# Prelu for the weights' words, v by pairs, zero products on the tensor engine and the softmax's factor on GpSimd

## The chip, the cores and the metric

One core of one Trainium2 chip runs the whole program. The metric is device time in microseconds of one execution, the median over the runs.

## The reference, cut to what matters

An attention layer whose heads are mixed before and after the softmax, followed by two dense pairs of layers. Sizes: 2 batches, 12 heads, 448 positions, head width 64; then 896 rows of 768, inner width 2048.

```python
scores = scale * np.matmul(q, k.transpose(0, 1, 3, 2))
scores = np.einsum('bhij,hg->bgij', scores, w_pre)
scores = scores - np.max(scores, axis=-1, keepdims=True)
attn = np.exp(scores)
attn = attn / (np.sum(attn, axis=-1, keepdims=True) + 1e-09)
attn = np.einsum('bhij,hg->bgij', attn, w_post)
return np.matmul(attn, v)
...
h = x @ w_in                              # first pair
g = np.where(h > 0.0, h, alpha * (np.exp(np.minimum(h, 0.0)) - 1.0))
y = g @ w_out
h = y @ w2_in                             # second pair
g = h * (1.0 / (1.0 + np.exp(-h)))
return g @ w2_out
```

The dense layers' weights arrive as float64: each is two 32-bit words, and the chip has to make a float32 of them before it can multiply.

## The kernel before, in words

The program has two stages, written out by hand in the order in which each engine is to run it.

**Attention.** The 896 rows of queries are cut into 8 tiles T (four per batch, of up to 120 rows), each tile into blocks of 10 rows; there are 90 blocks. Scores of a tile are made per pair of heads (`qk_pair`, tile `pq`), moved to SBUF (`qk_evac`, `s`) and from there laid out anew by a DMA per block (`relayout`, `blk`), so that 10 rows of 12 heads stand on 120 partitions. A block then goes through: `premix` on TensorE (mix with w_pre, tile `pre`), `rmax` on VectorE (`nmx`), `exps` on ScalarE (`pe`, with the row sums `sum`), `recip` on VectorE (add 1e-9, reciprocal, and `kr`, which is the post-mix matrix times the reciprocal: the softmax's factor), `postmix` on TensorE with `kr` (tile `post`), `post_hi` on ScalarE and `post_lo` on VectorE (two float16 parts, tile `a`). After a tile, `av_head` multiplies with v. v is also held in two float16 parts, which need a common scale: `v_max` takes a maximum per pair of heads, `v_scale` makes the scale of them in three steps (with two small matmuls, `vpa` and `vpb`), `prep_v` makes the parts: the high on ScalarE, the low either on VectorE (`v_lo`) or, in two operations, on GpSimd. `av_swap` sends half of a result to the other partitions by DMA and `av_sum` adds it, on GpSimd.

A loop over steps s records, in each step, `premix` of block s, `recip` of s-1, `postmix` of s-2 and `post_hi`, `post_lo` of s-3. Every engine works off its own list in order, so an instruction that waits holds all behind it on its engine. What else goes into a step stands in tables of steps: V_AT for v's work, P_AT for the two small matmuls, D_AT for DMAs (all issued by SP, also in order). Step 0 begins when the first tile's scores are made. Buffers: three PSUM banks for `pre`, two for `post`, one pair of banks for `pq`; five `blk`; two `s`.

**Dense layers.** From the last tile on, weights come in chunks: `load_w`, `scale_w` (ScalarE scales the high word), `bits_w` (VectorE joins the words by shifts and masks), `split_hi` on ScalarE and `split_lo` make two parts of 768 columns. The first three chunks (`n < NE`) are converted during the attention's last tile, with the tile `early` as their buffer, and their `split_lo` runs on GpSimd; all others on VectorE. Each product takes three matmuls (hi·hi, hi·lo, lo·hi).

The names in the rows: `vraw` and `vr` are raw v, `vmx` its maxima, `wr` and `wc` weights before and after the joining, `we` their parts, `ph`, `po`, `py` the products of the dense layers, `ptq` and `ptk` transposes of q and k, `xs`, `xt`, `xr` the attention's result.

## Time and profile before

| | |
|---|---|
| median of 3 runs | 743.95 us (743.8 to 744.45) |
| the profiled execution | 746.99 us, of which the span is 745.2 us |
| TensorE matmul | 722.4 us busy, 97% |
| TensorE weight load | 616.4 us, 83% |
| VectorE | 516.2 us, 69% |
| ScalarE | 398.1 us, 53% |
| GpSimd | 74.7 us, 10% |

The page divides the span into 40 slices of 18.6 us; digits are tenths. Matmuls overlap, so that the row of TensorE is at 9 even where single matmuls wait a little. Attention takes about the first 272 us; the last tile's result and the first dense products meet at about 270 to 282 us; from there to the end the dense layers run.

### The profile page before, as it was taken

How to read it: one execution, taken by the hardware profiler on the slowest of the kernel's cores; microseconds unless marked ns; L12 is line 12 of the kernel's file. 1: busy time of each engine (PE TensorE's matmuls, PEld its weight loads, DVE VectorE, ACT ScalarE, POOL GpSimd, SP SyncE). 2: the span in 40 equal slices, each digit the busy share in tenths (PEclk: the TensorE clock that was granted, in tenths of full speed). 3: DMA queues.
4: the chain of work that ended last, by engine and by line, in shares of the span. 5: the costliest groups of instructions: out<-in, count | busy, mean ns of one | idle time of the engine just before them, and what ended most of it. 6: DMA issues, size and time to landing. Idle time of an engine off the chain costs nothing.

```text
span 745.2 us, 12122 instructions
## 1 busy us (share of the span) xinstructions
PE 722.4 (97%) x4472; PEld 616.4 (83%) x4472; DVE 516.2 (69%) x1147; ACT 398.1 (53%) x789; POOL 74.7 (10%) x99
## 2 busy tenths in 40 slices
PE   7889999999998899999999999999999999999998
PEld 4456766776775688999999999999999999999997
DVE  5687877677776868888885556567888888833800
ACT  5577767788775657666663223335555555312301
POOL 1033011355123320000000000000000000000000
PEclk9899999999999999999999999999999999999999
DMA  6724735344325233333333333342333334633402
GB/s 121 219 82 130 188 103 146 117 122 142 105 95 173 81 114 106 105 109 107 106 102 104 113 113 113 113 127 83 110 104 108 106 107 119 183 102 106 139 1 74
DMA packets 90435, 85.70 MB, mean 115 GB/s; under 512 B 32664, under 2 KB 86280, under 8 KB 90376
## 3 DMA queue, kind: packets, MB, share of 16 engines
q1 hardware_dynamic: 90376, 84.93, 39.0%
q8 instruction: 35, 0.57, 0.3%
q14 instruction: 24, 0.20, 0.1%
HBM read 60.05 MB, written 2.75 MB: 84 GB/s over the span
## 4 chain that ended last, share of the span: by engine, by line
PE 90%; DVE 5%; DMA 3%; SPq 1%; ACT 1%; issue 0%; ACTq 0%
PE ph L716 30%; PE po L769 16%; PE post L352 9%; PE pre L310 7%; PE py L791 5%; PE py L789 5%; PE py L790 5%; PE pq L268 4%; PE av L385 4%; PE ph_mm L716 1%; DVE a L366 1%; DVE nmx L318 1%; DMA vraw<-in_v_dram 1%; DMA xs<-xt 1%; DVE kr L341 1%; PE ptk L151 1%
## 5 line engine op out<-in xcount | busy, mean ns | idle before, releaser
L716 PE MATMUL ph<-x,we 128*128 128x448 f32 x1116 | 231.0, 369 | 2.5 <-ACT x L559 1.5
L716 PEld LDWEIGHTS ph<-x,we 128*128 128x128 f32 x1116 | 210.7, 189 | 22.2 <-ACT x L559 1.8
L352 PE MATMUL post<-kr,pe 120*112 120x120 f32 x720 | 93.8, 273 | 9.0 <-DVE a L366 8.5
L769 PE MATMUL po<-g,we 128*128 128x448 f32 x468 | 101.5, 366 | 0.0
L352 PEld LDWEIGHTS post<-kr,pe 120*112 120x112 f32 x720 | 80.5, 177 | 25.1 <-issue 17.7
L769 PEld LDWEIGHTS po<-g,we 128*128 128x128 f32 x468 | 87.8, 188 | 7.9
L328 ACT ACTIVATE pe<-pre,nmx 120x448 f32<-120x448 f32 x90 | 57.1, 634 | 62.9 <-DVE sum L338 54.2
L310 PE MATMUL pre<-blk,kpre 120*120 120x448 f32 x180 | 85.3, 556 | 2.4 <-DMA blk<-s 2.4
L318 DVE TENSOR_REDUCE nmx<-pre 120x1 f32<-120x448 f32 x90 | 55.9, 622 | 43.9 <-PE pre L310 43.6
L617 ACT ACTIVATE wr<-wr 128x384 f32<-128x384 f32 x126 | 67.3, 545 | 35.5 <-DMA wr<-in_moe_w_out_dram 31.2
L652 ACT CAST we<-wc 128x768 fp32r<-128x768 f32 (+1 forms) x63 | 51.0, 809 | 41.8 <-PE py L791 22.3
L659 DVE TENSOR_TENSOR we<-wc,we 128x768 fp32r<-128x768 f32 (+1 forms) x63 | 58.6, 930 | 19.5 <-ACT we L652 16.7
L632 DVE SCALAR_TENSOR_TENSOR wc<-wr,wc 128x384 int32<-128x384 int32 x126 | 68.8, 546 | 4.3
L634 DVE SCALAR_TENSOR_TENSOR wc<-wr,wc 128x384 int32<-128x384 int32 x126 | 68.5, 543 | 3.3
L366 DVE TENSOR_TENSOR a<-post,a 112x480 f16<-112x480 f32 x90 | 58.5, 650 | 5.2 <-ACT a L361 5.2
L790 PE MATMUL py<-we,g 128*128 128x384 f32 x182 | 61.0, 335 | 0.0
L791 PE MATMUL py<-we,g 128*128 128x384 f32 x182 | 61.0, 335 | 0.0
L789 PE MATMUL py<-we,g 128*128 128x384 f32 x182 | 61.0, 335 | 0.0
L385 PEld LDWEIGHTS <-v 112*128 112x128 f16 x768 | 42.2, 99 | 20.5 <-issue 18.3
L361 ACT ACTIVATE a<-post 112x480 f16<-112x480 f32 x90 | 51.6, 573 | 6.5 <-PE post L352 6.5
L385 PE MATMUL av<-a,v 112*128 112x120 f16 (+1 forms) x768 | 46.0, 215 | 0.9 <-DVE a L366 0.9
L268 PEld LDWEIGHTS pq<-kt,qt 64*120 64x120 f32 (+1 forms) x288 | 21.9, 175 | 29.2 <-ACT a L361 11.2
(111 smaller groups left out, 866.6 us busy)
## 6 DMA issues: line engine op xcount, KB each, us to landing
wr<-in_moe_w_in_dram SPq DMA_DIRECT2D x58, 384.0 KB
wr<-in_moe_w_out_dram SPq DMA_DIRECT2D x56, 384.0 KB
blk<-s SPq DMA_DIRECT2D x90, 210.0 KB
wr<-in_moe_w_out_dram SPq DMA_DIRECT2D x12, 256.0 KB
vr<-in_v_dram SPq DMA_DIRECT2D x12, 224.0 KB
out_dram<-y SPq DMA_DIRECT2D x14, 192.0 KB
early<-in_moe_w_in_dram SPq DMA_DIRECT2D x6, 384.0 KB
xs<-xt SPq DMA_DIRECT2D x36, 60.0 KB
```

What stands on the lines that cost most here:

```text
L310: nc.tensor.matmul(t[:r], kpre[:r].rearrange("p i h -> p (i h)")[:, :r], blk.pop(n)[:r], start=True, stop=True)
L352: nc.tensor.matmul(t[:CP, j, :, :ni], pp[:r, j * CP:(j + 1) * CP], k[:r, :, :ni], start=True, stop=True)
L366: nc.vector.tensor_tensor(a[:, 1, :, :, i0:i0 + ni], pst.pop(n)[:CP, :, :, :ni], a[:, 0, :, :, i0:i0 + ni], op=ALU.subtract)
L385: nc.tensor.matmul(o, vt[:, j, h % 2, :], a[:, c, j, h, :m], start=(c == 0 and j == 0), stop=(c == 1 and j == 3))
L617: nc.scalar.activation(hf, hf, AF.Copy, scale=2.0 ** -112)
L632: nc.vector.scalar_tensor_tensor(cc, r[:, :, 1], -2147483648, cc, op0=ALU.bitwise_and, op1=ALU.bitwise_or)
L634: nc.vector.scalar_tensor_tensor(cc, r[:, :, 0], 29, cc, op0=ALU.logical_shift_right, op1=ALU.bitwise_or)
L716: nc.tensor.matmul(ph, wt[:, kk * P:(kk + 1) * P], xq[hf, kk][:, xi], start=(n_ == 0), stop=(n_ + 1 == len(terms)))
L769: nc.tensor.matmul(po, wt[:, kk * P:(kk + 1) * P], g_out1(k0 + kk, gi, hf), start=(k0 == 0 and n_ == 0), stop=(k0 + kn == KF and n_ == 3 * ...
L789: nc.tensor.matmul(py, gh, hi[:, w_], start=(kf == 0), stop=False)
L790: nc.tensor.matmul(py, gh, lo[:, w_], start=False, stop=False)
L791: nc.tensor.matmul(py, gl, hi[:, w_], start=False, stop=(kf == KF - 1))
```

## The change

1. **Zero products.** After the first tile's scores, 7 matmuls of zeros (`keep(0)`) run on TensorE, then the transposes of the next queries, then 9 more (`keep(1)`).
2. **pq of the first tile** is two tiles of one bank each instead of one tile of two banks.
3. **v by pairs.** v of batch 0 is no longer loaded whole by three DMAs at step 0, but by pairs of heads into two buffers, twice: once for the maxima, once for the parts. The steps are spread: maxima at steps 2, 4, 6, 8, 9, 10 (before 1 to 6), scale at 10 to 12 (before 7 to 9), parts at 13, 15, ... 23 (before 9 to 12). For batch 1 maxima are at 26 to 36 (before 18 to 28), the scale at 38 to 40 (before 30 to 32).
4. **v's low parts** are all made by VectorE, in one operation per head.
5. **kr** is made by GpSimd.
6. **The words.** ScalarE's scaling of the high word is a parametric relu whose slope for negative numbers carries the sign bit along; VectorE joins the words in two operations instead of three.
7. **Low parts of the first three chunks** are made by VectorE, one step later.
8. **Order in a step.** The small matmuls (P_AT) come after `exps` instead of ahead of `post_hi`; relayouts have a table of their own (R_AT), run ahead of D_AT.

```diff
+NKEEP = (7, 9)
...
+    def load_v(b, p):
+
+        raw = bp.tile([CP, 2, 4, D], F32, name=f"vr{b}_{p}", tag="vr", bufs=2)
+        nc.sync.dma_start(raw, v[b, 2 * p:2 * p + 2].rearrange("h (p r) d -> p h r d", r=4))
+        vraw[b, p] = raw
...
-            if b or p % 2:
-                full = ap_.tile([CP, 4, D], F32, name=f"vf{p}_{e}", tag="vf", bufs=2)
-                nc.gpsimd.tensor_scalar(full, raw[:, e], sc, None, op0=ALU.mult)
-                nc.gpsimd.tensor_tensor(lo, full, hi, op=ALU.subtract)
-            else:
-                vev.append((lo, raw[:, e], sc, hi))
+            vev.append((lo, raw[:, e], sc, hi))
...
-        nc.vector.tensor_scalar(t[:r], mix["kps"][:r], q[:r], None, op0=ALU.mult)
+        nc.gpsimd.tensor_scalar(t[:r], mix["kps"][:r], q[:r], None, op0=ALU.mult)
...
+    def keep(i):
+        t = ps.tile([P, S], F32, name=f"keep{i}", tag="pre", bufs=PREB)
+        for _ in range(NKEEP[i]):
+            nc.tensor.matmul(t, wz[:, :P], wz, start=True, stop=True)
+
+    keep(0)
     transpose_q(1, 0)
     transpose_q(1, 1)
+    keep(1)
...
-        at(V_AT, 1 + p, lambda p=p: v_max(0, p))
-        at(V_AT, 9 + 0.7 * p, lambda p=p: prep_v(0, p))
...
+        at(V_AT, (2, 4, 6, 8, 9, 10)[p], lambda p=p: v_max(0, p))
...
-        nc.scalar.activation(hf, hf, AF.Copy, scale=2.0 ** -112)
+        nc.scalar.activation(hf, hf, AF.Prelu, scale=2.0 ** -112, alpha=2.0 ** 32)
...
             if 0 in ops:
-                nc.vector.tensor_scalar(cc, r[:, :, 1], 3, 0x7FFFFFFF, op0=ALU.logical_shift_left, op1=ALU.bitwise_and)
+                nc.vector.tensor_scalar(cc, r[:, :, 0], 29, None, op0=ALU.logical_shift_right)
             if 1 in ops:
-                nc.vector.scalar_tensor_tensor(cc, r[:, :, 1], -2147483648, cc, op0=ALU.bitwise_and, op1=ALU.bitwise_or)
-            if 2 in ops:
-                nc.vector.scalar_tensor_tensor(cc, r[:, :, 0], 29, cc, op0=ALU.logical_shift_right, op1=ALU.bitwise_or)
+                nc.vector.scalar_tensor_tensor(cc, r[:, :, 1], 3, cc, op0=ALU.logical_shift_left, op1=ALU.bitwise_or)
...
-        eng = nc.gpsimd if n < NE else nc.vector
-        eng.tensor_tensor(lo[:, :tot], cf[:, :tot], hi[:, :tot], op=ALU.subtract)
+        nc.vector.tensor_tensor(lo[:, :tot], cf[:, :tot], hi[:, :tot], op=ALU.subtract)
```

On TensorE, between the first tile's last scores (`pq_5`) and the first block, the order before is:

```order
L268 MATMUL pq_5_239<-kt_5_227,qt_137 120x448 x6
L163 MATMUL ptq_0_262<-ident,q_83 128x120 x3
L163 MATMUL ptq_1_267<-ident,q_83 128x120 x3
L310 MATMUL pre_291<-blk_248,kpre 120x448
L268 MATMUL pq_0_294<-kt_0_145,qt_266 120x448 x6
```

and now:

```order
L262 MATMUL pq_5_1_245<-kt_5_231,qt_137 120x448
L453 LDWEIGHTS wz
L453 MATMUL keep_268<-wz 128x448
...
L164 MATMUL ptq_0_276<-ident,q_83 128x120 x3
L164 MATMUL ptq_1_281<-ident,q_83 128x120 x3
L453 LDWEIGHTS wz
L453 MATMUL keep_285<-wz 128x448
...
L304 MATMUL pre_315<-blk_254,kpre 120x448
L262 MATMUL pq_0_318<-kt_0_145,qt_280 120x448 x6
```

Sixteen products of zeros now stand around the two transposes; what follows them is in the same order.

On VectorE, in the first three steps of the attention loop, the order before is:

```order
L318 TENSOR_REDUCE nmx_301<-pre_291 120x1
L318 TENSOR_REDUCE nmx_321<-pre_312 120x1
L338 TENSOR_SCALAR sum_304<-sum_304 120x1
L339 RECIPROCAL sum_304<-sum_304 120x1
L341 TENSOR_SCALAR kr_325<-kps,sum_304 120x120
L202 TENSOR_REDUCE vmx_331<-vraw_308 112x1
L318 TENSOR_REDUCE nmx_344<-pre_335 120x1
L338 TENSOR_SCALAR sum_328<-sum_328 120x1
L339 RECIPROCAL sum_328<-sum_328 120x1
L341 TENSOR_SCALAR kr_348<-kps,sum_328 120x120
L202 TENSOR_REDUCE vmx_331<-vraw_308 112x1
```

and now:

```order
L312 TENSOR_REDUCE nmx_325<-pre_315 120x1
L312 TENSOR_REDUCE nmx_345<-pre_336 120x1
L332 TENSOR_SCALAR sum_328<-sum_328 120x1
L333 RECIPROCAL sum_328<-sum_328 120x1
L312 TENSOR_REDUCE nmx_366<-pre_357 120x1
L332 TENSOR_SCALAR sum_352<-sum_352 120x1
L333 RECIPROCAL sum_352<-sum_352 120x1
L198 TENSOR_REDUCE vmx_381<-vr_0_332 112x1
L312 TENSOR_REDUCE nmx_391<-pre_387 120x1
```

The first maximum of v stands behind the third block's `nmx` instead of the second's, the second maximum is two steps later, and `kr` is gone from this engine.

On VectorE, where the first weights are joined during the last tile (two steps, from one half of a chunk to the next), the order before is:

```order
L630 TENSOR_SCALAR early<-early 128x384
L632 SCALAR_TENSOR_TENSOR early<-early 128x384
L634 SCALAR_TENSOR_TENSOR early<-early 128x384
L318 TENSOR_REDUCE nmx_3326<-pre_3323 120x1
L338 TENSOR_SCALAR sum_3313<-sum_3313 120x1
L339 RECIPROCAL sum_3313<-sum_3313 120x1
L341 TENSOR_SCALAR kr_3330<-kps,sum_3313 120x120
L366 TENSOR_TENSOR a_2967<-post_3307,a_2967 112x48x10
L318 TENSOR_REDUCE nmx_3365<-pre_3362 120x1
```

and now:

```order
L633 TENSOR_SCALAR early<-early 128x384
L635 SCALAR_TENSOR_TENSOR early<-early 128x384
L312 TENSOR_REDUCE nmx_3332<-pre_3329 120x1
L332 TENSOR_SCALAR sum_3320<-sum_3320 120x1
L333 RECIPROCAL sum_3320<-sum_3320 120x1
L360 TENSOR_TENSOR a_2975<-post_3314,a_2975 112x48x10
L312 TENSOR_REDUCE nmx_3370<-pre_3367 120x1
L332 TENSOR_SCALAR sum_3361<-sum_3361 120x1
L333 RECIPROCAL sum_3361<-sum_3361 120x1
L360 TENSOR_TENSOR a_2975<-post_3355,a_2975 112x48x10
L655 TENSOR_TENSOR we_3365<-early,we_3365 128x768
```

A joining has one operation fewer, `kr` is gone, and the chunk's low part (`we`) has come to this engine.

## Rows read from the trace of the kernel before

**Rows 1.** The page: granted TensorE clock in 40 slices, tenths of full speed.
```profile
PEclk9899999999999999999999999999999999999999
```

**Rows 2.** Windows: length, busy us of PE, PEld, DVE, ACT, POOL; PEclk; DMA; GB/s.
```profile
20.00:25.00 5.00, 5.00 (x12) 1.78 (x14) 0.77 (x3) 1.64 (x3) 0.00 (x0) 0.50 0.87 221
...
27.90:61.20 33.30, 29.05 (x178) 18.24 (x177) 29.80 (x86) 25.56 (x59) 10.69 (x13) 1.00 0.30 104
...
400.00:500.00 100.00, 100.00 (x491) 91.76 (x490) 56.66 (x115) 30.83 (x55) 0.00 (x0) 1.00 0.37 110
```

**Rows 3.** Timeline of TensorE around step 0: start us, us, what, [idle before <-releaser].
```profile
13.62 2.03 PE L268 MATMUL pq<-kt,qt 64*120 64x448 f32 x12
16.69 0.81 PE L163 MATMUL ptq<-ident,q 120*128 120x120 f32 x6 [1.04 <-DMA q<-in_q_dram]
19.87 1.82 PE L310 MATMUL pre<-blk,kpre 120*120 120x448 f32 x2 [2.37 <-DMA blk<-s]
...
27.95 1.07 PE L352 MATMUL post<-kr,pe 120*112 120x120 f32 x8
...
61.18 1.00 PE L385 MATMUL av<-a,v 112*128 112x120 f16 x16
```

**Rows 4.** Timeline of VectorE, first maximum of v.
```profile
28.42 0.69 DVE L202 TENSOR_REDUCE vmx<-vraw 112x1 f32<-112x512 f32 x1 [2.31 <-DMA vraw<-in_v_dram]
```

**Rows 5.** Groups of VectorE, 27.9 to 61.2 us: busy us, mean ns, idle before.
```profile
L341 DVE TENSOR_SCALAR kr<-kps,sum 120x120 f32<-120x120 f32 x13 | 4.5, 342 | 0.5
L202 DVE TENSOR_REDUCE vmx<-vraw 112x1 f32<-112x512 f32 x6 | 4.1, 678 | 2.3 <-DMA vraw<-in_v_dram 2.3
L232 DVE SCALAR_TENSOR_TENSOR v<-vraw,sc_v,v 112x256 f16<-112x256 f32 x6 | 3.4, 615 | 0.0
```

**Rows 6.** Chain of waits, steps with little waiting (60 to 125 us).
```profile
68.83 0.80 PE pq L268 x6
69.63 1.00 PE post L352 x8
70.63 0.75 PE pre L310 x2
...
124.77 0.82 PE post L352 x8
```

**Rows 7.** Timeline of TensorE at 111 us.
```profile
110.98 0.60 PE L151 MATMUL ptk<-ident,kr 112*128 112x112 f32 x4 [0.98 <-ACT s L278]
```

**Rows 8.** Waits of TensorE, 238 to 252 us: total us, times, longest.
```profile
PE post L352 <- DVE a L366: 1.9, 2, 1.6
PE av L385 <- DVE a L366: 0.9, 1, 0.9
```

**Rows 9.** Groups of the whole run: weights' operations.
```profile
L617 ACT ACTIVATE wr<-wr 128x384 f32<-128x384 f32 x126 | 67.3, 545 | 35.5 <-DMA wr<-in_moe_w_out_dram 31.2 <-DMA wr<-in_moe_w_in_dram 4.3
...
L634 DVE SCALAR_TENSOR_TENSOR early<-early 128x384 int32<-128x384 int32 x6 | 3.4, 558 | 0.2
...
L731 ACT ACT_TABLE_LOAD x1 | 1.3, 1283 | 0.0
```

**Rows 10.** Timeline of VectorE and GpSimd at 244 us.
```profile
244.70 1.60 DVE L341 TENSOR_SCALAR kr<-kps,sum 120x120 f32<-120x120 f32 x1
...
244.40 1.82 POOL L659 TENSOR_TENSOR we<-early,we 128x768 fp32r<-128x768 f32 x1 [3.22 <-DVE nmx L318]
```

**Rows 11.** Groups of GpSimd, shapes apart.
```profile
L418 POOL TENSOR_TENSOR xr<-xt,xs 64x240 f32<-64x240 f32 x18 | 12.7, 707 | 94.2 <-DMA xs<-xt 70.4 <-ACT pe L328 16.4 <-ACT a L361 7.4
...
L247 POOL TENSOR_SCALAR vf<-vr,sc_v 112x256 f32<-112x256 f32 x12 | 11.2, 932 | 0.4
```

**Rows 12.** Timelines at 223 to 225 us: one block's kr, and its post.
```profile
222.94 0.28 DVE L341 TENSOR_SCALAR kr<-kps,sum 120x120 f32<-120x120 f32 x1
...
225.15 1.07 PE L352 MATMUL post<-kr,pe 120*112 120x120 f32 x8
```

**Rows 13.** Timeline of ScalarE at 231 us.
```profile
230.62 0.54 ACT L617 ACTIVATE early<-early 128x384 f32<-128x384 f32 x1 [3.90 <-DMA blk<-s]
```

More of the change, by code (lines that the diff above doesn't have):

```diff
@@ L200, in v_max @@
             vmx[b] = cp.tile([CP, NP], F32, name=f"vmx{b}")
-        raw = vraw[0][:, 2 * p:2 * p + 2] if b == 0 else vraw[1, p]
-        nc.vector.tensor_reduce(vmx[b][:, p:p + 1], raw.rearrange("p h r d -> p (h r d)"), axis=AX.X, op=ALU.max, apply_absolute_value=True)
+        nc.vector.tensor_reduce(vmx[b][:, p:p + 1], vraw[b, p].rearrange("p h r d -> p (h r d)"), axis=AX.X, op=ALU.max, apply_absolute_value=True)
     vst = {}
@@ L239, in prep_v @@
         sc = vs[b][0][:CP]
-        raw = vraw[0][:, 2 * p:2 * p + 2] if b == 0 else vraw[1, p]
+        raw = vraw[b, p]
         for e in range(2):
@@ L263, in qk_pair @@
         qt, kt = qT[T][:, :, p], kT[b, p]
-        pq = psp[0].tile([P, 2, 512], F32, name=f"pq{T}_{p}", tag="mm", bufs=2 if T == 0 else 1)[:m, :, :S]
+        if T == 0:
+            pq = [p0.tile([P, S], F32, name=f"pq0_{p}_{e}", tag=f"mm{e}", bufs=2)[:m] for e in range(2)]
+        else:
+            pq = psp[0].tile([P, 2, 512], F32, name=f"pq{T}_{p}", tag="mm", bufs=1)[:m, :, :S]
         for n, (i, j) in enumerate(((0, 0), (0, 1), (1, 0))):
@@ L267, in qk_pair @@
                 half = slice(e * D, (e + 1) * D)
-                nc.tensor.matmul(pq[:, e], qt[half, i, :m], kt[half, j, :], start=(n == 0), stop=(n == 2))
+                nc.tensor.matmul(pq[e] if T == 0 else pq[:, e], qt[half, i, :m], kt[half, j, :], start=(n == 0), stop=(n == 2))
         sev.append((T, p, m, pq))
@@ L274, in qk_evac @@
             if T == 0:
-                nc.scalar.activation(o[:, 0], pq[:, 0], AF.Copy, scale=0.125)
-                nc.vector.tensor_scalar(o[:, 1], pq[:, 1], 0.125, None, op0=ALU.mult)
+                nc.scalar.activation(o[:, 0], pq[0], AF.Copy, scale=0.125)
+                nc.vector.tensor_scalar(o[:, 1], pq[1], 0.125, None, op0=ALU.mult)
             else:
@@ L497, in attn_moe_moe @@
                 at(V_AT, v1[p], lambda p=p, b=b: prep_v(b + 1, p))
-                at(D_AT, l - 5 + p if p < 2 else v1[p - 2] + 2, lambda p=p: load_v1(p))
+                at(D_AT, l - 5 + p if p < 2 else v1[p - 2] + 2, lambda p=p: load_v(1, p))
     for n in range(NBLK, last[0] + 1):
-        at(D_AT, n - NBLK + 1, lambda n=n: relayout(n))
-    for g in range(3):
-        at(D_AT, 0, lambda g=g: load_v0(g))
+        at(R_AT, n - NBLK + 1, lambda n=n: relayout(n))
     for p in range(NP):
-        at(V_AT, 1 + p, lambda p=p: v_max(0, p))
-        at(V_AT, 9 + 0.7 * p, lambda p=p: prep_v(0, p))
-        at(D_AT, 16 + 2 * p, lambda p=p: load_v1(p))
-        at(V_AT, 18 + 2 * p, lambda p=p: v_max(1, p))
-    for b, st in ((0, 7), (1, 30)):
+        at(D_AT, max(0, 2 * p - 2), lambda p=p: load_v(0, p))
+        at(V_AT, (2, 4, 6, 8, 9, 10)[p], lambda p=p: v_max(0, p))
+        at(D_AT, 10 + 2 * p, lambda p=p: load_v(0, p))
+        at(V_AT, 13 + 2 * p, lambda p=p: prep_v(0, p))
+        at(D_AT, 24 + 2 * p, lambda p=p: load_v(1, p))
+        at(V_AT, 26 + 2 * p, lambda p=p: v_max(1, p))
+    for b, st in ((0, 10), (1, 38)):
         for i in range(3):
@@ L522, in step @@
         run(QK_AT, s)
-        run(P_AT, s)
         do(post_hi, s - LAG[1])
@@ L535, in step @@
         do(exps, s)
+        run(P_AT, s)
         transpose_hi()
@@ L539, in step @@
         run(V_AT, s)
+        run(R_AT, s)
         run(D_AT, s)
@@ L616, in scale_w, with bits_w @@
         hf = rawt[n][j][0][:, :, 1].bitcast(F32)
-        nc.scalar.activation(hf, hf, AF.Copy, scale=2.0 ** -112)
-    def bits_w(n, part=None, ops=(0, 1, 2)):
+        nc.scalar.activation(hf, hf, AF.Prelu, scale=2.0 ** -112, alpha=2.0 ** 32)
+    def bits_w(n, part=None, ops=(0, 1)):
         tl = rawt[n]
```

25 lines of the change are left out of this document (7 added, 18 removed).

## The prediction

> **What bounds the kernel now.** I read the page's clock line first, then a table of windows, then the waits and timelines of the stretches in which TensorE is not full. In the dense layers the window of 400 to 500 us shows TensorE busy for 100.00 of 100 us with 491 products, 0.204 us each, while VectorE has 57 us of work and ScalarE 31 [rows 2]. Whatever the change takes from those two there is worth nothing, since nobody waits for them. What can be won lies ahead of 290 us, where the clock line has its few eights [rows 1] and where waits of TensorE are listed. There are four places.
>
> First, the start. The first tile's scores end at 13.62 + 2.03 = 15.65 us; the transposes wait until 16.69, the first block's transfer lands at 19.87 [rows 3]. After that gap the granted clock is 0.50, that is 1.2 GHz, in the window from 20 to 25 us [rows 2]; it is back at 2.4 GHz in the stretch behind it, whose mean is 1.00.
>
> Second, the first tile's steps, 27.95 to 61.18 us [rows 3]. Here VectorE bounds: 29.80 us busy in a window of 33.30 [rows 2], and it begins by waiting 2.31 us for v [rows 4], with the next block's `nmx` behind.
>
> Third, one wait of 0.98 us at 111 us [rows 7]. Just ahead of it VectorE ran the small operations of batch 1's scale in front of `nmx`, so that ScalarE's exponential and evacuation came late.
>
> Fourth, the last tile, where weights are joined: TensorE waits 1.9 + 0.9 us for `post_lo` [rows 8], again because VectorE is late.
>
> A fifth stall, around 231 us, is ScalarE standing 3.90 us in front of the first scaling of weights until a transfer lands [rows 13], with `post_hi` behind it. The change touches neither that instruction's place nor the loads ahead of it: I leave it in.
>
> **The change part by part.**
>
> *Zero products.* 16 at 0.204 us (the pace in rows 2) are 3.3 us of TensorE. Seven take 15.65 to 17.08, so that the transposes start 0.4 us later than at 16.69; they need 0.81, to 17.89; nine more end at 19.73, just under the landing at 19.87 [rows 3]. So they lie in the gap and push nothing. If the gap keeps the clock up, the 5.1 us from 19.87 to 25 at half speed shrink by at most 2.6. I take 2.4, because the single pair of `pq` banks, which ScalarE has to empty, will hold a product now and then. Below: 0 if the clock falls all the same, and -3.1 if the zeros themselves ran at half speed (15.65 + 16 x 0.41 + 0.81 = 23.0 instead of 19.87).
>
> *v by pairs, kr off VectorE, v's parts later.* The first tile's work for TensorE between 27.95 and 61.18 counts 13 `post`, 13 `pre`, 6 `pq`, and about 1.2 us of transposes and scale products. Undisturbed, a `post` takes 1.00 behind a `pq` and 0.82 otherwise, a `pre` 0.75, a `pq` 0.80 [rows 6]. 7 x 1.00 + 6 x 0.82 + 13 x 0.75 + 6 x 0.80 + 1.2 = 27.7 us, against 61.18 - 27.95 = 33.2: 5.5 us is all that can be won. Does VectorE allow it? Of its 29.8 us, `kr` (4.5) and v's low parts (3.4) leave the stretch, the maxima (4.1) stay [rows 5]: 21.9, below 27.7. So TensorE becomes the bound. I take 5.0, keeping 0.5 for the first maximum: it now stands one step later, behind a load half as large, but if v lands at 28.42 as before, the fourth block's `nmx` is late by over a us. Bounds: 2.3 (only the wait for v goes) and 5.5. v's low parts return in the second tile, two operations of 0.615 [rows 5] in every second step, where a step has an `av` beside the rest; the order leaves room and I charge nothing (2 us if not). The second loading of v adds 6 transfers of 224 KB. A load waits for the low part made two steps earlier and holds the relayouts behind it on SP; these run four steps ahead of use, so nothing (2 us, one step, if that lead is gone).
>
> *kr on GpSimd.* 90 instructions. No row has it there: the nearest is 0.932 for 256 columns with a per-row factor, VectorE's own 0.28 for these 120 columns is the other end [rows 11, 12]. I take 0.5, near the proportion 120/256 with something fixed on top. Between the start of `kr` and its `post` lie 225.15 - 222.94 = 2.2 us [rows 12], so even 0.93 is hidden there (the first tile's steps, without `av`, leave less); queued behind it on GpSimd is only the sum of `xr`, whose reader is a whole tile away. On VectorE `kr` met GpSimd: one took 1.60 us beside a GpSimd operation of 1.82 [rows 10], instead of 0.28. The Trainium skill, GPSIMD Engine Reference, section Specifications, says that the two share their SBUF interface and collide when VectorE runs in a two-port mode or has two SBUF inputs; the 1.60 us agree. By that rule v's low parts on VectorE can be held by `kr` on GpSimd: a rival below.
>
> *The scale of v behind `exps`.* The 0.98 us at 111 [rows 7] go: 1.0. Bounds 0 and 1.0.
>
> *The words during the last tile.* Per half chunk VectorE loses one operation of 0.558 [rows 9] and per block a `kr` that took 0.28 to 1.60; it gains three low parts, for which I take half of GpSimd's 1.82, as a two-input operation. In the four halves and seven blocks between 236 and 252 us that is at least 2.2 + 2.0 off and 1.8 on. What comes next in line is TensorE itself, so of the 2.8 us of waits [rows 8] I take 2.7. Bounds 1 and 2.8.
>
> *Prelu for Copy.* No row has it; the nearest is 0.545 for the Copy of the same shape [rows 9]. I take the same. Twice that would add 126 x 0.545 = 69 us to ScalarE over some 455 us of dense layers, 15 in 100, to the 31 that it has [rows 2]: still hidden, so nothing either way. A table load took 1.283 us [rows 9]. The changed program has two of them on ScalarE, as the one before has. The Trainium skill, ScalarE: Activation LUTs, section Table sets, says that a function of another set costs a reload at every change of set; by that 132 scalings between exponentials would bring up to 264 loads, some 340 us. The program's order shows that none is issued, so the sum has none.
>
> *Single-bank pq of the first tile, and the rest of the words:* nothing, under TensorE's own pace; 0.5 us either way at the start.
>
> The sum: 2.4 + 5.0 + 1.0 + 2.7 = 11.1 us. The profiled execution took 746.99 (span 745.2), so it would be 735.9 with the change; the median of the runs, 743.95, lies 3.0 below that execution, and the forecast on that footing is 743.95 - 11.1 = 732.9.
>
> **The rivals.**
>
> *The start is not won.* The clock falls in spite of the zeros, or v lands late and stops VectorE as before. For it: the gaps between the new pieces, and that v's load still queues behind a query load and five relayouts. Against it: the engine is given work for all but about 0.2 us of the gap. Then 2.4 goes and the first tile keeps half: 743.95 - 2.5 - 3.7 = 737.8.
>
> *Collisions with GpSimd.* One collision of up to 0.5 us in each of the 20 or so steps that have v's parts or weights on VectorE is 10 us of VectorE; half may reach TensorE: 743.95 - 11.1 + 5 = 737.9. For it: the 1.60 us [rows 10]. Against it: `kr` is short, and the victims have slack.
>
> *GpSimd becomes the bound: slower.* The `xr` sums wait on GpSimd for their transfers, 70.4 us in all before 18 pairs [rows 11], and GpSimd works in order, so a `kr` behind a waiting sum is late, and its `post` on TensorE with all products behind it. With 2.2 us between `kr` and `post` [rows 12] and 0.5 for `kr`, it begins to hurt when the sums end 1.7 us after the reciprocal. It decides the sign when 18 pairs cost more than 11.1 / 18 = 0.62 us each; at 2 us each the time is 743.95 - 11.1 + 36 = 769. Against it: that step's own `kr` stands ahead of the sums, so a transfer has a whole step, some 2.5 us, before the next `kr`; most of the 70.4 us is an engine with nothing else to do.
>
> *Given back.* The attention ends 11 us earlier, but the fifth stall and the exchange before the dense layers grow because transfers, not TensorE, pace them: 743.95. For it, the 3.90 us [rows 13]; against it, those transfers are issued only after relayouts that follow TensorE, so they move forward too.
>
> **How the numbers follow.** Forecast 0.62, start not won 0.14, collisions 0.12, given back 0.05, GpSimd the bound 0.07. The measurement tells apart about 0.2%, 1.5 us. The first three are faster by more than that: 0.88; given back is the same: 0.05; slower 0.07. The lower end, 729, is the full bounds (2.6 + 5.5 + 1.0 + 2.8 = 11.9) and part of the fifth stall; the upper, 740, is either of the first two rivals with 2 us more, such as one of the 2 us put at nothing above. Outside lie the last two cases and a little more.
>
> **What would show it.** After the change: clock 1.00 from 15 to 30 us, the first `post` at about 25.5 us instead of 27.95, the first `av` near 54; no wait for v on VectorE over 1 us; no 0.98 us wait at the fourth tile's end; in the last tile no TensorE wait over 1 us for `post_lo` except that behind ScalarE's wait for weights; `kr` about 0.5 us on GpSimd and no `post` waiting for it; dense layers at 0.204 us per product as before. I am wrong if `post` or SP waits on GpSimd in many steps, if the clock still dips at 20 us, or if the second tile shows new waits for ScalarE or VectorE.

## The result, and the profile after

The changed kernel took 734.69 us (median; 731.37 to 736.34) beside 743.88 us of the kernel before in the same session: a ratio of 0.9863, interval 0.9831 to 0.9896. Run again in a later session, with six executions instead of four, it took 731.48 us (729.95 to 737.81) beside 746.24: 0.9813, interval 0.9772 to 0.9855. Ratios and intervals are of fast runs, as recorded (one slow execution of the kernel before, 886.59 us, is left out of them), and are not quite the quotients of the medians. The forecast was 732.9 in a range of 729 to 740, a ratio of 0.985, which lies in both intervals. The profiled execution took 731.37 us, the shortest of its session; its span is 729.6.

The page of the changed kernel has nines in every slice of the granted clock, where [rows 1] had one eight:

```profile
PEclk9999999999999999999999999999999999999999
```

TensorE's timeline at the start of the changed kernel answers to [rows 3] (start us, us, what):

```profile
15.10 0.67 PE L262 MATMUL pq<-kt,qt 64*120 64x448 f32 x4 [0.20 <-DVE kt L179]
15.70 1.50 PE L453 MATMUL keep<-wz 128*128 128x448 f16 x7
17.04 0.78 PE L164 MATMUL ptq<-ident,q 120*128 120x120 f32 x6
17.66 1.87 PE L453 MATMUL keep<-wz 128*128 128x448 f16 x9
19.49 0.98 PE L304 MATMUL pre<-blk,kpre 120*120 120x448 f32 x2
...
25.44 1.07 PE L346 MATMUL post<-kr,pe 120*112 120x120 f32 x8
...
53.42 0.79 PE L379 MATMUL av<-a,v 112*128 112x120 f16 x12
```

The 16 zero products fill the gap; the first `post` starts at 25.44 (27.95 before), the first `av` at 53.42 (61.18). The windows of the same kernel (columns as in [rows 2]):

```profile
20.00:25.00 5.00, 4.41 (x22) 1.84 (x22) 2.18 (x7) 3.17 (x6) 0.58 (x1) 1.00 0.91 213
...
25.40:53.40 28.00, 27.92 (x177) 18.77 (x176) 22.84 (x67) 21.68 (x49) 8.31 (x14) 1.00 0.50 161
...
266.00:269.00 3.00, 3.00 (x10) 2.65 (x9) 2.64 (x5) 2.97 (x6) 0.00 (x0) 0.52 0.23 68
...
400.00:500.00 100.00, 100.00 (x491) 91.69 (x490) 41.79 (x84) 32.57 (x59) 0.00 (x0) 1.00 0.35 107
```

In the first tile TensorE is busy for 27.92 of 28.00 us, and VectorE for 22.84: the bound has moved to TensorE. The dense layers run 491 products in 100 us as before, with 15 us less work on VectorE, which nobody waited for. The third row is a stretch that the change leaves alone: after the exchange ahead of the dense layers, which sends the last attention results between partitions, the clock is at 0.52, 1.2 GHz, as it was before (0.52 from 281 to 284 us).

VectorE's timeline of the changed kernel at the first maximum of v, to set beside [rows 4]:

```profile
26.94 0.69 DVE L198 TENSOR_REDUCE vmx<-vr 112x1 f32<-112x512 f32 x1 [1.45 <-DMA vr<-in_v_dram]
```

The maximum starts 1.48 us earlier, and VectorE still stands 1.45 us for it, without TensorE waiting behind it. GpSimd's group of `kr` from 25.4 to 53.4 us (busy us, mean ns, idle before), beside the bounds of [rows 11, 12]:

```profile
L335 POOL TENSOR_SCALAR kr<-kps,sum 120x120 f32<-120x120 f32 x13 | 7.6, 583 | 20.5 <-DVE sum L333 20.5
```

It takes 0.58 us, and its idle time is waiting for the reciprocal. ScalarE's timeline at the first scaling of weights, which answers to [rows 13]:

```profile
219.29 0.56 ACT L621 ACTIVATE early<-early 128x384 f32<-128x384 f32 x1 [1.49 <-DMA blk<-s]
```

ScalarE waits 1.49 us for its transfer where it waited 3.90. In the last tile, 225 to 262 us, this is all that TensorE waits for (total, times, longest), against [rows 8]:

```profile
PE post L346 <- POOL kr L335: 0.5, 2, 0.4
```

Five marks, read from TensorE's timeline of the profiled executions, show where the time went (us; block 77 of the 90 stands shortly ahead of the first scaling of weights, `ph_mm` is the first product with weights beside the last tile, dense 60 the 61st product `ph` of the dense layers):

| kernel | first post | first av | block 77's pre | first ph_mm | dense 60 | span |
|---|---|---|---|---|---|---|
| before | 27.9 | 61.2 | 223.5 | 251.2 | 291.0 | 745.2 |
| changed | 25.4 | 53.4 | 214.6 | 236.0 | 275.4 | 729.6 |
| changed, again | 25.7 | 53.7 | 214.9 | 236.4 | 276.1 | 730.2 |
| 1 no zeros | 27.2 | 55.2 | 216.4 | 237.8 | 276.1 | 730.2 |
| 2 kr on VectorE | 26.0 | 54.4 | 216.3 | 238.8 | 278.8 | 734.9 |
| 3 three operations | 25.7 | 53.7 | 214.9 | 237.2 | 277.1 | 731.3 |
| 4 before, with zeros | 26.1 | 61.1 | 223.5 | 248.3 | 287.6 | 741.9 |
| 5 v as before | 25.7 | 63.4 | 228.8 | 250.5 | 289.8 | 746.0 |
| 6 v as before, low parts on VectorE | 26.0 | 61.9 | 223.3 | 244.4 | 285.9 | 740.2 |
| 7 small operations first | 25.8 | 55.5 | 216.6 | 238.1 | 276.3 | 728.2 |
| 8 kr twice | 25.5 | 54.4 | 215.8 | 240.1 | 278.2 | 732.3 |
| 9 scaling later | 25.7 | 53.7 | 214.9 | 235.4 | 275.2 | 729.4 |
| 10 load behind | 25.3 | 53.3 | 214.5 | 236.0 | 272.8 | 724.7 |
| 11 both orders | 25.9 | 53.9 | 215.1 | 235.6 | 272.5 | 726.7 |

Single runs of one kernel differ by several us (the changed kernel, run again: 729.95 to 737.81), so effects of 1 us are read from these marks and not from medians. The marks spread too: the first `post` starts at 25.3 to 25.9 us in seven traces of kernels that are the same up to there, while the stretch from it to the first `av` agrees within 0.02 us in six of the seven (run 7 has an edit in it). So a difference under half a us in a single mark says nothing, and distances between marks say more. There is one trace of each kernel.

### The profile page after: what moved, and what is told of

Read it like the earlier page. It is cut to its first block, busy times and chain, and to the rows that moved or that the text cites. A ratio compares the mean times of both kernels' runs of the same rounds, so it can differ in the third digit from the quotient of the medians.

```text
span 729.6 us, 12115 instructions
## 1 busy us (share of the span) xinstructions
PE 720.1 (99%) x4488; PEld 616.9 (85%) x4488; DVE 423.2 (58%) x946; ACT 396.0 (54%) x789; POOL 96.4 (13%) x150
## 4 chain that ended last, share of the span: by engine, by line
PE 97%; DVE 1%; DMA 1%; ACT 1%; POOL 0%; issue 0%; ACTq 0%; SPq 0%; POOLq 0%
PE ph L712 31%; PE po L765 16%; PE post L346 11%; PE pre L304 9%; PE py L787 5%; PE py L785 5%; PE py L786 5%; PE pq L262 5%; PE av L379 5%; PE ph_mm L712 1%; DMA xs<-xt 1%; PE warm L428 1%; PE ptq L164 1%; PE ptk L152 1%; PE keep L453 0%; POOL kr L335 0%
## 5 line engine op out<-in xcount | busy, mean ns | idle before, releaser
L621 ACT ACTIVATE wr<-wr 128x384 f32<-128x384 f32 x126 | 67.2, 544 | 29.9 <-DMA wr<-in_moe_w_out_dram 26.1
L304 PE MATMUL pre<-blk,kpre 120*120 120x448 f32 x180 | 83.1, 543 | 0.0
L335 POOL TENSOR_SCALAR kr<-kps,sum 120x120 f32<-120x120 f32 x90 | 57.5, 639 | 141.6 <-DVE sum L333 132.5
L635 DVE SCALAR_TENSOR_TENSOR wc<-wr,wc 128x384 int32<-128x384 int32 x126 | 68.6, 544 | 5.2
L727 ACT ACTIVATE e<-ph 128x448 f32<-128x448 f32 x32 | 17.4, 544 | 52.9 <-PE ph L712 52.9
```

The lines of the kernel that those rows point to most:

```text
L304: nc.tensor.matmul(t[:r], kpre[:r].rearrange("p i h -> p (i h)")[:, :r], blk.pop(n)[:r], start=True, stop=True)
L621: nc.scalar.activation(hf, hf, AF.Prelu, scale=2.0 ** -112, alpha=2.0 ** 32)
L635: nc.vector.scalar_tensor_tensor(cc, r[:, :, 1], 3, cc, op0=ALU.logical_shift_left, op1=ALU.bitwise_or)
```

## The experiments

The changed kernel itself, without an edit, beside the others.

> The changed kernel once more, as the measure for the others of this chip: 9 us shorter than before by the comparison already made, 11.1 by the sum. If the spread of its runs comes from the stall in front of the first scaling of weights, runs with a mean clock of 0.998 are near 731 us and those at 0.993 to 0.995 near 735 to 736, and the profile of a run of one sort shows that stall at about 0.7 us or at about 3 us with the clock at 1.2 GHz behind it.

731.48 us, ratio 0.9813 [0.9772, 0.9855]. Its marks agree with the first profile within 0.4 us up to the first `ph_mm`, and the runs below are compared with it. (They were measured in three sessions, in which the kernel before had medians of 746.53, 746.24 and 745.48, so that medians from different sessions compare within about 1 us.) What spreads its runs is not settled: ScalarE's wait at 219 us is 1.62 here with the clock at 1.00 behind it, and the one long run, 737.81 at a mean clock of 0.992, has no trace.

**1. Without the zero products.**

```
-    keep(0)
     transpose_q(1, 0)
     transpose_q(1, 1)
-    keep(1)
```

> The changed kernel without the 16 products of zeros. Theory of terms: the clock falls to 1.2 GHz again in the gap ahead of the first block, the window from 20 to 25 us shows about 0.50, the first post comes near 27.9 us instead of 25.4, and the time is 2.4 us longer than the changed kernel's (about 737 against 734.7). Rival: with v's load out of the way the gap is no longer what matters, the clock comes back early, and the time differs by less than 0.7 us.

731.96 us, 0.9817 [0.9782, 0.9851]: the median tells no difference. The windows of this kernel show the clock:

```profile
15.00:20.00 5.00, 1.90 (x13) 1.11 (x12) 3.45 (x12) 1.90 (x4) 0.00 (x0) 1.00 0.30 92
20.00:25.00 5.00, 5.00 (x17) 1.97 (x17) 1.68 (x5) 1.84 (x4) 0.00 (x0) 0.66 0.86 219
```

TensorE is busy for 1.90 of 5 us, and behind that the granted clock is 0.66 on average, part of the stretch at 1.2 GHz. The first `post` is 1.5 us later than with zeros, and every mark up to the first `ph_mm` keeps 1.3 to 1.5 (1.8 against the first profile). The theory had the cause right and the size, 2.4 us, too large. At dense 60 the lead is gone: in this execution the clock stayed up after the exchange ahead of the dense layers, and in the one with zeros it fell. The zeros are worth 1.5 us where nothing else intervenes, less than the medians can show.

**2. kr on VectorE.**

```
-        nc.gpsimd.tensor_scalar(t[:r], mix["kps"][:r], q[:r], None, op0=ALU.mult)
+        nc.vector.tensor_scalar(t[:r], mix["kps"][:r], q[:r], None, op0=ALU.mult)
```

> The changed kernel with kr back on VectorE. Theory of terms: in the first tile VectorE's work rises by 4.5 us, still below TensorE's 27.7 us there, so that the first av moves by under 0.5 us; in the last tile a wait for the low part of post returns in part. In all 0 to 1.5 us longer than the changed kernel. Rival: kr is what made VectorE the bound, and its return costs over 4 us. Second rival: GpSimd's kr costs more than it gives (two post wait for it in the profile, and single kr took 2 us beside weights' operations), and the time gets shorter by up to 1 us.

734.03 us, 0.9833 [0.9794, 0.9871]. By the marks it is 0.7 us behind at the first `av`, 1.4 at block 77 and 2.4 at the first `ph_mm`. Of each 0.3 is there at the first `post`, within the spread of the start; counted from there it loses 0.4, 1.1 and 2.1. The window of its first tile has VectorE, with `kr`, still below TensorE:

```profile
26.00:54.40 28.40, 28.06 (x177) 18.63 (x176) 26.05 (x80) 21.75 (x49) 0.00 (x0) 1.00 0.58 175
```

The waits of TensorE between 115 and 255 us of this kernel:

```profile
PE post L346 <- DVE a L360: 2.2, 3, 0.9
```

So `kr` off VectorE is worth 2.1 to 2.4 us up to the dense layers, in small pieces. The theory's 0 to 1.5 was too small for the last tile. (The span is 4.7 us longer than the changed kernel's; 1.9 of that come in the dense layers, with the pace of the last section.)

**3. Three operations on the weights' words, with Copy, as before.**

```
-        nc.scalar.activation(hf, hf, AF.Prelu, scale=2.0 ** -112, alpha=2.0 ** 32)
+        nc.scalar.activation(hf, hf, AF.Copy, scale=2.0 ** -112)
...
-                nc.vector.tensor_scalar(cc, r[:, :, 0], 29, None, op0=ALU.logical_shift_right)
+                nc.vector.tensor_scalar(cc, r[:, :, 1], 3, 0x7FFFFFFF, op0=ALU.logical_shift_left, op1=ALU.bitwise_and)
...
-                nc.vector.scalar_tensor_tensor(cc, r[:, :, 1], 3, cc, op0=ALU.logical_shift_left, op1=ALU.bitwise_or)
+                nc.vector.scalar_tensor_tensor(cc, r[:, :, 1], -2147483648, cc, op0=ALU.bitwise_and, op1=ALU.bitwise_or)
+            if 2 in ops:
+                nc.vector.scalar_tensor_tensor(cc, r[:, :, 0], 29, cc, op0=ALU.logical_shift_right, op1=ALU.bitwise_or)
...
```

> The changed kernel with the words joined as before (Copy on ScalarE, three operations on VectorE). Theory of terms: in the dense layers TensorE is the bound and nothing changes there; in the last tile six halves cost VectorE 0.56 us each again, without kr there is room, so TensorE's waits return by 0 to 1.5 us. In all 0 to 1.5 us longer than the changed kernel. Rival: the operation taken from every chunk is worth something in the dense layers, and 132 of them bring back over 3 us.

732.46 us, 0.9812 [0.9768, 0.9857]. All marks are equal up to block 77; the first `ph_mm` is 0.7 us later. The third operation costs 0.7 us in the last tile; from dense 60 to the end this trace and the changed kernel's take the same time, 454.2 and 454.1 us, so it costs nothing in the dense layers.

**4. The kernel before, with the zero products alone.** The edit is the function `keep` and its two calls, put into the kernel before.

> The kernel before with the products of zeros alone. Theory of terms: the clock stays at 2.4 GHz from 15 to 25 us, the second and third block come 2 us earlier, but VectorE then stands longer before v's load, which does not land sooner, so that the gain of 2.4 us is mostly eaten: 0 to 1 us shorter than before. Rival: the gain is independent of the rest, and the time is 2.4 us shorter.

743.95 us, 0.9973 [0.9948, 0.9998]. VectorE's first maximum of v in this kernel:

```profile
28.37 0.69 DVE L202 TENSOR_REDUCE vmx<-vraw 112x1 f32<-112x512 f32 x1 [4.22 <-DMA vraw<-in_v_dram]
```

The interval leaves a gain of 0.02 to 0.5% (up to 4 us), so by medians neither the theory's 0 to 1 us nor the rival's 2.4 is excluded; the marks say where it doesn't come from. The first `post` is 1.8 us earlier than before, and the first `av` at 61.1 is where it was. v lands at 28.4 in either kernel, so VectorE only waits longer, 4.22 us instead of 2.31 [rows 4]. Up to block 77 the zeros alone win nothing. The 2.9 us at the first `ph_mm` come behind that: here ScalarE stood 1.92 us ahead of its first scaling of weights, with no transfer named, and the clock stayed up. Whether the zeros have a part in that, one trace of each doesn't show. The window of 230 to 235 us of this kernel:

```profile
230.00:235.00 5.00, 4.26 (x36) 3.09 (x36) 4.79 (x13) 3.55 (x10) 1.14 (x1) 1.00 0.77 241
```

The same window of the kernel before, at a mean clock of 0.83 behind the wait of [rows 13]:

```profile
230.00:235.00 5.00, 2.54 (x12) 1.55 (x13) 3.24 (x8) 4.38 (x11) 1.14 (x1) 0.83 0.66 202
```

**5. v as before: loaded whole, prepared early, its low parts shared with GpSimd.** Batch 1's loads and steps are as before too; all else is as changed. Of the order, the core of the edit:

```
-        at(D_AT, max(0, 2 * p - 2), lambda p=p: load_v(0, p))
-        at(V_AT, (2, 4, 6, 8, 9, 10)[p], lambda p=p: v_max(0, p))
-        at(V_AT, 13 + 2 * p, lambda p=p: prep_v(0, p))
+        at(V_AT, 1 + p, lambda p=p: v_max(0, p))
+        at(V_AT, 9 + 0.7 * p, lambda p=p: prep_v(0, p))
```

> The changed kernel with v as before: batch 0 loaded whole at step 0, maxima at steps 1 to 6, scale at 7 to 9, parts at 9 to 12, every second low part on GpSimd; kr stays on GpSimd. Theory of terms: the wait of VectorE for v's load is back (over 2 us), and the first tile's maxima fall in its first six steps; without kr VectorE has 25 us of work beside TensorE's 27.7, so about 2 to 4 us of the 5 come back and the first av is near 57 us. Rival: kr alone made the room, v's place is worth under 1 us.

744.26 us, 0.998 [0.9953, 1.0006]: the whole gain is gone. Waits of TensorE from 25 to 66 us of this kernel:

```profile
PE post L356 <- POOL kr L345: 6.0, 3, 2.8
```

Its windows:

```profile
25.00:30.00 5.00, 2.48 (x16) 1.42 (x16) 1.86 (x5) 0.64 (x3) 0.32 (x1) 1.00 1.02 256
30.00:35.00 5.00, 4.68 (x21) 2.80 (x22) 4.17 (x11) 3.88 (x9) 1.43 (x3) 0.66 0.59 212
50.00:55.00 5.00, 3.21 (x10) 2.01 (x10) 4.08 (x10) 5.00 (x12) 3.88 (x6) 0.69 0.12 45
```

The releaser is `kr` on GpSimd, but that has two possible causes: GpSimd busy with v's low parts in front of it, or `kr` itself late behind a VectorE that waits for v. And behind the waits of 2.84 and 1.96 us the clock goes down (means of 0.66 and 0.69 in the second and third window), which it doesn't behind the third, of 1.24 us (1.00 from 62 to 68 us). The next run separates them.

**6. The same, with all low parts of v on VectorE,** so that GpSimd has only `kr` there:

```
-            if b or p % 2:
-                full = ap_.tile([CP, 4, D], F32, name=f"vf{p}_{e}", tag="vf", bufs=2)
-                nc.gpsimd.tensor_scalar(full, raw[:, e], sc, None, op0=ALU.mult)
-                nc.gpsimd.tensor_tensor(lo, full, hi, op=ALU.subtract)
-            else:
-                vev.append((lo, raw[:, e], sc, hi))
+            vev.append((lo, raw[:, e], sc, hi))
```

> The changed kernel with v loaded whole and prepared early in the first tile, as before the change, but with all of v's low parts on VectorE, so that GpSimd has only the factor operation there. It separates the two halves of the change to v: its place in the order and the engine of its low parts. Theory (in the run with v as before, the factor operation stood on GpSimd behind v's low parts): no wait of the first tile's products for GpSimd over 1 us; VectorE then has the maxima, and 12 low parts of 0.6 us, 7.4 us, where it had 3.4 before, less the 4.5 of the factor operation: the first attention product ends at about 58 to 60 us, between 53 and 62.6, and the time is about 737. Rival (v's place in the order decides, not GpSimd's queue): first attention product at 61 us or later, time 742 to 744 as in the run with v as before.

739.06 us, 0.9927 [0.9897, 0.9958]. The theory fell: the first `av` is at 61.9, 8.2 us behind the changed kernel's, and the wait for `kr` is still there with an empty GpSimd. Waits of TensorE from 25 to 66 us of this kernel:

```profile
PE post L351 <- POOL kr L340: 4.6, 3, 3.2
PE post L351 <- DVE a L365: 1.2, 2, 0.8
```

VectorE's timeline at its first maximum of v:

```profile
28.82 0.69 DVE L203 TENSOR_REDUCE vmx<-vraw 112x1 f32<-112x512 f32 x1 [5.16 <-DMA vraw<-in_v_dram]
```

The 5.16 us of VectorE for v hold back the sum behind them, that holds back `kr`, and TensorE stands 3.23 us. So v's place (its whole load and its early steps, which were not taken apart) decides 8.2 of the 9.7 us of run 5 at the first `av`. The low parts on GpSimd add 1.5 there, and 5.5 by block 77, since in run 5 TensorE waits another 3.6 us for `kr` between 66 us and block 77; the rival's time, 742 to 744, was too high for that reason. Run 4, with `kr` on VectorE and v in its old place, has its first `av` at 61.1, earlier than runs 5 and 6 with `kr` on GpSimd: there the relief bought nothing, since `kr` stood behind v's low parts (run 5) or these took its room on VectorE (run 6).

**7. The small operations of v's scale ahead of the exponential again.**

```
         run(QK_AT, s)
+        run(P_AT, s)
         do(post_hi, s - LAG[1])
...
         do(exps, s)
-        run(P_AT, s)
```

> The changed kernel with the small operations of v's scale back ahead of the step's score mixing and exponential on each engine, as before the change. Theory (they stand in front of the row maxima on VectorE at 111 us of the kernel before, and cost 0.98 us there): TensorE waits about 1 us once in the fourth tile, time about 732.5, 1 us over the changed kernel; no other place. Rival (with pairs of v and later steps the small operations meet no full VectorE): no wait, same time within 0.5 us.

731.62 us, 0.9826 [0.9788, 0.9863]; the median tells no difference. The marks lose 1.8 us, all of it by the first `av`, and keep 1.7 up to the first `ph_mm`; at dense 60 only 0.2 is left, because the clock stayed up after the exchange (run 10). Waits of TensorE from 25 to 115 us of this kernel:

```profile
PE vpa L209 <- DVE vma L206: 0.9, 1, 0.9
PE post L346 <- POOL kr L335: 0.9, 1, 0.9
```

Both lie in the first tile, at 46 and 51 us, where batch 0's scale is made. At the fourth tile's end nobody waits. The expectation had the size nearly right and the place wrong.

**8. kr executed twice on GpSimd.**

```
+        nc.gpsimd.tensor_scalar(t[:r], mix["kps"][:r], q[:r], None, op0=ALU.mult)
         nc.gpsimd.tensor_scalar(t[:r], mix["kps"][:r], q[:r], None, op0=ALU.mult)
```

> The changed kernel with the factor operation executed twice on GpSimd, with the same operands and output, 90 instructions of 0.58 us more. Theory (the operation has slack between its reciprocal and the products that read it, except in the first tile's steps, which have no attention product): hidden behind the first tile; there at most 0.2 us for each of 13 steps, in all 0 to 3 us, time 731 to 734. Rival (TensorE waits for it in every step, and it is on the path): 90 times some 0.3 us or more, 27 us, time about 758.

734.16 us, 0.9845 [0.9812, 0.9878], 2.7 us over the changed kernel for 90 x 0.58 = 52 us more work. Waits of TensorE from 25 to 262 us of this kernel:

```profile
PE post L347 <- POOL kr L336: 2.1, 6, 1.0
PE post L347 <- DVE a L361: 1.8, 1, 1.8
```

Six waits in 90: `kr` has slack nearly everywhere. 0.7 us are lost by the first `av`, as expected; 2.7 us more between block 77 and the first `ph_mm`, which the theory did not name. Of these 1.0 is the wait of 1.8 us for `post_lo`, where the changed kernel waits 0.8: ScalarE stands 2.66 us ahead of its first scaling of weights here, not 1.62, for a transfer of weights. Another 1.0 are longer waits for `kr`. Whether the second `kr` has a part in ScalarE's stall is open.

**9. The first scaling of weights one step later.**

```
-            at(M_AT, ft - 4 + 4 * n + 2 * j, lambda n=n, j=j: scale_w(n, j))
+            at(M_AT, ft - 4 + 4 * n + 2 * j + (n + j == 0), lambda n=n, j=j: scale_w(n, j))
```

> The changed kernel with the first scaling of weights one step later, so that ScalarE passes post's high part before it stands in front of that transfer. If the stall of the changed kernel at 219 us (1.5 us of ScalarE in the profiled run, 3.9 in the kernel before) is what spreads its runs: all runs near 731, mean clock 0.998, 2 to 4 us shorter than the changed kernel's median. Rival: the spread comes from elsewhere (start, end), and only 0 to 0.7 us goes.

730.64 us, 0.9789 [0.9754, 0.9824]. ScalarE's scaling in this kernel:

```profile
220.20 0.56 ACT L621 ACTIVATE early<-early 128x384 f32<-128x384 f32 x1
```

It waits for nothing, TensorE's wait of 0.8 us behind it is gone, and the first `ph_mm` is 1.0 us earlier. The median is 0.8 us shorter and the runs still spread from 728.66 to 732.99, so the rival is nearer than the theory; that this stall is the source of the spread is not shown.

**10. The fifth chunk of weights loaded behind the last exchange,** not ahead of it.

```
-    load_w(NE + 1)
     for h in range(H):
...
             av_swap()
+    load_w(NE + 1)
     for j in range(2):
```

> The changed kernel with the load of the fifth chunk of weights issued behind the last exchange of attention results instead of ahead of it. If the exchange (about 5 us from its first issue to the first sum) is late because 768 KB stand ahead of it: it lands 1.5 to 2.5 us sooner, TensorE's gap before the dense layers falls from about 3 us to about 1 and the clock does not fall behind it: 2 to 4 us shorter than the changed kernel. Rival: the exchange's own latency bounds it and nothing moves; second rival: the fifth chunk is then late and costs 1 to 3 us.

727.54 us, 0.9756 [0.9718, 0.9793]. TensorE's timeline at the exchange, of the changed kernel run again:

```profile
261.77 1.40 PE L712 MATMUL ph<-x,we 128*128 128x448 f32 x6
264.75 0.47 PE L712 MATMUL ph<-x,we 128*128 128x448 f32 x1 [1.58 <-ACT x L562]
266.23 2.24 PE L712 MATMUL ph<-x,we 128*128 128x448 f32 x5 [1.00 <-DVE x L567]
```

The same of this kernel:

```profile
261.74 1.17 PE L712 MATMUL ph<-x,we 128*128 128x448 f32 x5
264.43 3.90 PE L712 MATMUL ph<-x,we 128*128 128x448 f32 x18 [1.51 <-DVE x L567]
```

One wait instead of two, 1.5 us instead of 2.6. Behind the two waits the window of the changed kernel, run again, has the clock at 0.50, 1.2 GHz:

```profile
266.00:269.00 3.00, 2.77 (x7) 2.51 (x8) 2.66 (x7) 2.94 (x7) 0.00 (x0) 0.50 0.05 12
```

Behind the one wait this kernel's window has it at 1.00:

```profile
266.00:269.00 3.00, 3.00 (x17) 2.78 (x16) 2.66 (x5) 3.00 (x7) 0.00 (x0) 1.00 0.89 299
```

From the first `ph_mm` to dense 60 that is 2.8 us. But the clock does not always fall behind the two waits. Run 7, with the order of the changed kernel here, has both between 260 and 290 us:

```profile
PE ph L712 <- ACT x L562: 1.6, 1, 1.6
PE ph L712 <- DVE x L567: 1.0, 1, 1.0
```

and behind them the clock at 1.00:

```profile
268.00:270.00 2.00, 2.00 (x11) 1.85 (x12) 1.73 (x6) 1.94 (x5) 0.00 (x0) 1.00 0.00 0
```

From the first `ph_mm` to dense 60 the changed kernel takes 39.6 us, runs 1 and 7 with the clock up 38.3 and 38.2, run 10 takes 36.8. So about 1.4 us of the gain are the wait that is gone and about 1.4 the clock, which some executions keep without the edit. All six runs of this kernel have a mean clock of 1.000, three of the six of the changed kernel. The other 2.3 of the spans' difference come in the dense layers, which no edit touched (last section); that differs between executions. So of the 3.9 us between the medians the marks give at most 2.8 to the edit.

**11. Both orders.** The edits of 9 and 10 together.

> The changed kernel with two orders altered: the first scaling of weights by ScalarE stands one step later, and the fifth chunk of weights is loaded behind the last exchange before the dense layers instead of ahead of it. Theory (both waits are of transfers, and independent): the load's place is worth about 4 us as in the run with it alone (727.5 against 731.5), the later scaling another 1 us, in all about 726.5, with the granted clock at 1.00 in every stretch from 15 us to the end and no wait of TensorE over 1.5 us behind 20 us. Rival (the wait in front of the scaling only moves, since the same transfer is waited for by the operation behind it): 727.5, no different from the load's place alone.

726.13 us (725.36 to 728.41), 0.9741 [0.9707, 0.9775], the best version of this study. The expected 726.5 came out; its wait at the exchange is 1.6 us, a little over the 1.5 expected. At dense 60 it is 3.6 us ahead of the changed kernel and only 0.3 ahead of run 10; but its start is 0.6 us later than run 10's. From the first `post` to dense 60 it takes 246.6 us, the changed kernel 250.3, run 9 249.5 and run 10 247.5: 3.7 us are gained where the two edits alone gain 0.8 and 2.8. By the marks the two add up, as the theory has it; the medians, 726.13 and 727.54 in different sessions, don't show the second.

## Why the prediction was right, point by point

**Start: 2.4 forecast, 2.2 to 2.5 measured, but not a term by itself.** Without zeros the clock is down for part of 20 to 25 us, with them it is at 1.00, as forecast. (The "few eights" that the prediction reads in [rows 1] are one.) Run 1 prices the zeros at 1.5 of the 2.2. The rest is there without them: in run 1 the windows of one us show the clock down from 20.4 to 23.8 us, and before the change from 18.3 to 25.1. Whether the change shortens that (the single-bank `pq` has no run of its own) or the execution, one trace of each doesn't show. Run 4 shows that in the old order the whole of it is given back to the wait for v. So the rival "start is not won" was the truth for the zeros without the change to v; the sum added two terms that hold only together.

**First tile: 7.4 forecast together with the start, 7.5 to 7.8 measured.** From the first `post` to the first `av` the change takes 5.2 us off, where the sum had 5.0. TensorE became the bound, busy 27.92 of 28.00 us beside the estimate of 27.7 for its work. But the two reliefs of VectorE weigh differently from their busy times: `kr`, 4.5 us of VectorE [rows 5], is worth 0.4 to 0.7 us there (run 2), and v's place 8.2 (run 6), more than the whole 7.5, since run 6 reaches the first `av` 0.7 us later than the kernel before. Without v's low parts VectorE's 29.80 [rows 2] less 3.4 [rows 5] is 26.4; run 2 measured 26.05 beside TensorE's 28.06. That is already below TensorE, and a relief below that buys little. My sign "no wait for v on VectorE over 1 us" was wrong, at 1.45; TensorE has no wait from 25 to 66 us all the same.

**The wait at 111 us: 1.0 forecast, gone, for another reason.** It is absent in run 7, which has the small operations in their old place with the later steps, and in run 6, which has the old steps behind the exponential: with `kr` on GpSimd, as in both, either is enough. Run 2 has `kr` on VectorE and both other changes, and has no wait there either. Whether `kr` off VectorE is enough by itself no run shows. The place behind the exponential pays 1.8 us in the first tile instead, which no term of the forecast named. Between first `av` and block 77 the changed kernel gains 1.2 us on the one before, the forecast 1.0.

**Last tile: 2.7 forecast, 6.2 to 6.3 measured between block 77 and the first `ph_mm`.** The step that failed is "a fifth stall ... I leave it in". The waits of TensorE in the kernel before, 223 to 252 us:

```profile
PE post L352 <- DVE a L366: 4.9, 3, 3.0
PE av L385 <- DVE a L366: 0.9, 1, 0.9
```

The 3.0 is the wait behind ScalarE's stall of 3.90 [rows 13]; behind it four us run at a clock of 0.57:

```profile
233.00:237.00 4.00, 4.00 (x27) 2.98 (x27) 3.83 (x10) 2.55 (x7) 0.96 (x1) 0.57 0.31 90
```

In the changed kernel the same wait is 0.65 (0.77 run again), behind a stall of 1.49 (1.62), and the clock stays at 1.00. That is 2.3 us of waiting and an estimate of 1.7 us of clock (4 us at 0.57 do the work of 2.3), about 4.0 in all, where the sum had nothing. The waits that the forecast named, 2.8 us [rows 8], left 0.5 for `kr`: 2.2 to 2.3 gained of the 2.7. Together that is the 6.2 to 6.3. Whether the change itself shortens the stall is open. Run 4, with the old order, has it at 1.92, and its stretch takes 24.8 us instead of 27.7. In the eleven other traces in which the first scaling keeps its step, ScalarE stands 1.17 to 2.66 us ahead of it, so the 3.90 from which the forecast started may have been a long one.

Against run 4's stretch 3.3 to 3.4 us are gained, near the 2.7: its waits other than that behind the scaling are 3.3 us in all, and 0.5 are left. Of these gains, run 2 puts 1.0 to `kr` (2.4 at `ph_mm` less 1.4 at block 77) and run 3 puts 0.7 to the third operation; where the other 1.6 come from was not separated, v's low parts off GpSimd and the low part of the weights on VectorE being candidates.

**Put at nothing.** Prelu took 544 ns where Copy took 545 [rows 9], with two table loads as before. The dense layers kept their 491 products in 400 to 500 us. v's parts in the second tile brought no wait. `kr` at 0.58 us, where I took 0.5, is waited for 0.5 us in all. The relayouts ahead of other transfers have no run of their own.

**The rivals.** "GpSimd becomes the bound" fell: `post` waits for `kr` twice in 90 blocks, and with twice the work (run 8) six times. "Collisions" exist and do not matter: one `kr` took 2.07 us (below), and its `post` waited 0.4. "Given back" fell: from dense 60 to the end the marks lead by 14.9 to 15.6 us in the profiled executions. By medians the gain is 9.2 us in the first session and 14.8 in the second, around the forecast of 11.1. That the sum comes so near is in part luck: by the marks the start and the first tile are right, the last tile is short by 3.5, and the executions of one kernel spread by as much as that.

## What to carry to other kernels

An engine's busy time prices a relief only down to the point where the next engine bounds: here v's place, with 3.4 us off VectorE and the wait that went with them, decided, and the next 4.5 were worth 0.4 to 0.7. A stall seen in one trace may be longer there than it mostly is: the 3.90 us of one trace stand against 1.17 to 2.66 in eleven others. Work pulled forward in front of a transfer that does not move is given back to that transfer, so test each term in the old order as well as taking it out of the new one. A releaser named in the waits may be only the last in a row: `kr` on GpSimd held TensorE because VectorE, in front of it, stood for a load.
